# Two weight loads, fifteen narrow matmuls and a table split moved in a retention-plus-feed-forward kernel

## The chip, the core and the metric

The kernel runs on one core of a Trainium2 chip. The metric is the device time of one execution in microseconds (us). Three executions of the kernel before took 202.52, 202.65 and 206.85 us; their median is 202.65 us.

## The reference

Two parts follow each other. The first is a recurrent attention with a decaying state, for 4 batches, 8 heads, 768 steps and a head size of 64. The second is a feed-forward layer over its 3072 rows, with a slope `alpha` for negative values.

```python
gamma = 1 - 2 ** (-5 - arange(H))
for t in range(S):
    state = gamma * state + outer(k[:, :, t], v[:, :, t])
    y[:, :, t] = scale * (q[:, :, t] @ state)
x = y.transpose(0, 2, 1, 3).reshape(3072, 512)
h = x @ w_in                                   # 512 -> 2048
out = (maximum(h, 0) + alpha * minimum(h, 0)) @ w_out   # 2048 -> 512
```

## The kernel before, in words

The 3072 rows are cut into twelve units of 256 rows (three to a batch), and two units make a block, so there are six blocks. Five engines run their own instruction lists in the written order and wait for each other by semaphores: TensorE (PE), VectorE (DVE), ScalarE (ACT), GpSimd (POOL) and SyncE (SP). The schedule is written out by hand: the order of the calls in the source is the order on each engine.

For one unit, `load` (L129) issues DMAs for k, q and v from SP. `rescale` (L166) multiplies k or q by powers of gamma and writes fp16 tiles `kdq`; `cast_v` (L179) makes `vx` from v. Either runs on the engine that the call names (V is DVE, G is POOL). `turn_pe` (L191, through PE and ACT) or `turn_dma` (L187, a transposing DMA from SP) gives the transposed `kq`. `sum_mm` (L218) forms the sums of k times v, `state_sum` (L245) and `state_copy` (L259) the running state `tg`. `score_mm` (L272) multiplies k by q, `masks` (L293) masks the result on DVE, and `out_mm` (L310) multiplies states and masked scores into `y`, which `take_y` (L351) copies out as `xT`.

A block of two units then goes through `ffn1` (L393): sixteen tiles of 128 columns of `w_in`, each four matmuls deep over a moving operand of 512 columns. For the first `apart` tiles the two units go separately, with 256 columns each, two tiles to a bank; a matmul of 256 columns is called narrow here. ACT makes `hm` from each finished bank, DVE combines both into `gt`. Block 0 ends in a plain product `ffn2` (L436), whose four stores are issued from SP at L459 as soon as each result is copied out; later blocks use a product of seven half-size parts (`ffn2_seven`, L462), for which `w_sums` (L370) builds sums of `w_out` quarters once, and `g_sums` (L380) sums of `gt` for each block. Both `ffn` functions are generators: `tick(gen, m)` (L569) issues m more matmuls of one, and this is how the attention of the next units is woven between them.

The weights are loaded from POOL's own DMA queue, in four pieces each: `get_wi(lo, hi)` (L577) and `get_wo(i)` (L581). The DMA converts them from fp32 to fp16. One piece of `w_in` holds four tiles. `behind` (L105) makes one instruction wait for another; `hold` (L115) makes the next plain load wait for the instruction that was last put into `held`.

`SPLIT` (L41) is the unit from which another layout is used: rows of a pair of steps lie 64 apart instead of next to each other. From there on, k and v are loaded by four DMAs each, in rows of 64 numbers instead of 128 (L139 to L147, which does not go through `hold`), half of the score and value matmuls have 64 columns instead of 128 (L282, L336), and the masks have 384 columns instead of 512 (L296).

At the start, DVE rescales unit 0 (L617 to L620), POOL casts its v (L621), issues the first piece of `w_in` (L622) and rescales half of unit 1's q (L623). The second piece is issued at L646, behind POOL's share of the state. `ffn1` of block 0 begins at L668 with seven narrow matmuls ahead of unit 1's `out_mm` (L677).

Of the kernel before, what the change touches and what calls it, by code (L numbers as in the profile page):

```python
# [12 lines left out]
SUB = mybir.AluOpType.subtract  # L13
# [8 lines left out]
def kernel(  # L22
# [10 lines left out]
    nc = tc.nc  # L33
# [4 lines left out]

    SPLIT = 6  # L41
    U = 256
    UPB = S // U
    NU = B * UPB
# [42 lines left out]
    HF, HM = NFT // 2, d_model // 2  # L87
# [5 lines left out]
    def keep(m, bank=7):  # L93
        pt = ps(bank, "kps")
        for i in range(m):
            nc.tensor.matmul(
                out=pt, lhsT=spin[:, 0:128], rhs=spin, start=True, stop=True
            )
# [1 line left out]
    tgbuf = [sbp.tile([128, NP, 128], F16, tag=f"tg{i}", name=f"tg{i}") for i in range(6)]  # L100

    staged, prepped, live, tgs, xT, gts, gsums = {}, {}, {}, {}, {}, {}, {}
    held = []

    def behind(ins, other):  # L105
        tc.add_manual_dep(
            ins.ins,
            other.ins.name,
            mybir.DependencyInfo(
                mybir.DependencyClass.Sync, mybir.DependencyReason.DATA  # L110
            ),
            reason="one engine of two at the second read port",
        )

    def hold(ins):  # L115
# [50 lines left out]
    def rescale(eng, u, t, h0, h1):  # L166
        kdq = unit(u)[0]
        at = OQ if t else (O2 if u >= SPLIT else 0)
        return eng.tensor_tensor(  # L169
            out=kdq[:, t, :, h0:h1, :].rearrange("p r h d -> p h r d"),  # L170
            in0=staged[u]["kq"[t]][:, h0:h1, :].rearrange("p h (r d) -> p h r d", r=2),
            in1=tab[:, at + 2 * h0 : at + 2 * h1]
            .rearrange("p (h r) -> p h r", r=2)
            .unsqueeze(3)
            .to_broadcast([128, h1 - h0, 2, D]),
            op=MULT,
        )

    def cast_v(eng, u, h0=0, h1=H):  # L179
        o = unit(u)[2][:, h0:h1].rearrange("p h r d -> p (h r d)")  # L180
        i = staged[u]["v"][:, h0:h1].rearrange("p h x -> p (h x)")
        if eng is nc.scalar:
            eng.activation(out=o, in_=i, func=COPY, bias=0.0, scale=1.0)
        else:
            eng.tensor_copy(out=o, in_=i)  # L185

    def turn_dma(u):  # L187
        kdq, kq, _ = unit(u)
        nc.sync.dma_start_transpose(out=kq, in_=kdq.rearrange("p t r h d -> p (t r h d)"))
# [51 lines left out]
    def state(u, c, eng, copy="gg"):  # L241

        state_copy(state_sum(u, c, eng), copy)
# [49 lines left out]
    def masks(u, hh, parts=(0, 1)):  # L293
        for a in parts:
            m2 = sbp.tile([128, 512], F16, tag=f"m2{a}{hh}", bufs=2, name=f"m2{a}{hh}")
            if u >= SPLIT:  # L296
                i = nc.vector.tensor_tensor(
                    out=m2[:, 0:384], in0=live[u, hh][a][:, 0:384], in1=mj, op=MULT
                )
            else:  # L300
                i = nc.vector.tensor_tensor(  # L301
                    out=m2.rearrange("p (r a i) -> p r a i", r=2, a=2),
                    in0=live[u, hh][a].rearrange("p (r a i) -> p r a i", r=2, a=2),
                    in1=mask.unsqueeze(2).to_broadcast([128, 2, 2, 128]),
                    op=MULT,
                )
            live[u, hh][a] = m2
        return i
# [58 lines left out]
                scale=1.0,  # L367
            )

    def w_sums(i, lo, hi):  # L370

        w = w_out_all.rearrange("p (k f) (j e) -> p k f j e", k=2, j=2)
        w12, w21, w22 = w[:, 0, lo:hi, 1, :], w[:, 1, lo:hi, 0, :], w[:, 1, lo:hi, 1, :]
        t1, t2, t3, t4 = (wsum[:, x, lo:hi, :] for x in range(4))
        o, a, b = (
            (t1, w12, w[:, 0, lo:hi, 0, :]), (t2, w22, t1), (t3, w22, w12), (t4, w21, t2)
        )[i]
        return nc.vector.tensor_tensor(out=o, in0=a, in1=b, op=SUB)

    def g_sums(n, i, lo, hi):  # L380

# [54 lines left out]
    def ffn2(n, banks, parts=1):  # L436
        gt = gts.pop(n)
        opss = {}
        step = NFT // parts
        for f0 in range(0, NFT, step):  # L440
            for tq in range(4):
                if f0 == 0:
                    opss[tq] = ps(banks[tq % len(banks)], "ops")
                for ft in range(f0, f0 + step):
                    nc.tensor.matmul(  # L445
                        out=opss[tq],
                        lhsT=gt[:, ft, 128 * tq : 128 * tq + 128],
                        rhs=w_out_all[:, ft, :],
                        start=(ft == 0),
                        stop=(ft == NFT - 1),  # L450
                    )
                    if ft == NFT - 1:
                        tag = ("os", "cu")[tq % 2]
                        os_sb = sbp.tile([128, d_model], FP, tag=tag, bufs=3, name=tag)
                        nc.scalar.activation(
                            out=os_sb, in_=opss[tq], func=COPY, bias=0.0, scale=1.0
                        )
                        row = TB * n + 128 * tq
                        nc.sync.dma_start(out=out[row : row + 128, :], in_=os_sb)  # L459
                    yield  # L460

    def ffn2_seven(n, x, y, z=None):  # L462
# [106 lines left out]
    def tick(gen, m=10**6):  # L569
        for _ in range(m):  # L570
            if next(gen, 1) == 1:
                return
# [4 lines left out]
    def get_wi(lo, hi):  # L577
        s = slice(128 * lo, 128 * hi)
        return nc.gpsimd.dma_start(out=w_in_all[:, :, s], in_=wi[:, :, s])
# [37 lines left out]
    rescale(V, 0, 0, 0, 4)  # L617
    rescale(V, 0, 1, 0, 4)
    rescale(V, 0, 0, 4, 8)
    rescale(V, 0, 1, 4, 8)  # L620
    cast_v(G, 0)  # L621
    get_wi(0, 4)  # L622
    rescale(G, 1, 1, 0, 4)  # L623
    keep(10)
    turn_pe(0, 0, 0)
    keep(2)
# [16 lines left out]
    state(0, 0, V, "aa")  # L643
    masks(0, 1, (1,))
    s01 = state_sum(0, 1, G)
    held.append(get_wi(4, 8))  # L646
    load(2, ("k0", "q0", "k1", "q1", "v"))
    rescale(V, 1, 0, 4, 8)
    rescale(V, 1, 1, 4, 8)
# [15 lines left out]
    score_mm(1, 1, (0, 1))  # L665
    masks(1, 1)
    state(1, 1, G)
    gen = ffn1(0, (2, 3, 6, 7, 0, 1, 2, 3, 6, 7, 4, 5, 0, 1, 2, 3), apart=4)  # L668
    tick(gen, 7)
    get_wo(0)  # L670
    rescale(G, 2, 0, 0, 4)
    get_wo(1)
    rescale(G, 2, 1, 0, 4)
    rescale(G, 2, 0, 4, 8)
    rescale(G, 2, 1, 4, 8)
    cast_v(G, 2)
    out_mm(1, (4, 5), evict=False)  # L677
    take_y(1, (0,))
# [7 lines left out]
    turn_pe(2, 0, 5)  # L686
    tick(gen, 5)
    score_mm(2, 0, (6, 7))
    held.append(masks(2, 0, (0,)))
    load(3, ("k0", "q0", "k1", "q1", "v"))  # L690
    masks(2, 0, (1,))
    turn_pe(2, 1, 4)
    tick(gen, 6)
    score_mm(2, 1, (6, 7))
# [3 lines left out]
    held.append(get_wo(2))  # L698
    load(4)
    load(5)  # L700
    rescale(V, 3, 0, 0, 4)
    rescale(G, 3, 1, 0, 4)
    get_wo(3)
    rescale(V, 3, 0, 4, 8)
    rescale(G, 3, 1, 4, 8)
    cast_v(G, 3)
    w_sums(0, 0, HF)
    tick(gen, 9)
    out_mm(2, (4, 5))
    tick(gen, 7)  # L710
# [11 lines left out]
    tick(gen, 8)  # L722
    score_mm(3, 1, (4, 5))
    masks(3, 1)
    state(3, 1, G)
    for f in (0, 4):
        for i in range(1, 4):
            gate = w_sums(i, f, f + 4)
    behind(rescale(G, 4, 1, 0, 8), gate)
    rescale(G, 5, 0, 0, 8)  # L730
    rescale(G, 5, 1, 0, 8)
    cast_v(G, 4)
    cast_v(G, 5)
    tick(gen, 8)
    out_mm(3, (6, 7))
    tick(gen)
    turn_dma(4)
    turn_dma(5)
    load(6)
    tick(half)  # L740
# [2 lines left out]
    for n in range(1, NBLK):  # L743
        more = n + 1 < NBLK
        u0 = 2 * (n + 1)
        if n > 1:
            gen = ffn1(n, (7, 2, 3, 1, 0, 6, 5, 4, 7, 1, 0, 4, 5, 6, 7, 1))
            if more:
                for u in (u0, u0 + 1):
                    i = rescale(G, u, 0, 0, 8)  # L750
                    if u == u0:
                        behind(i, gate)
                    rescale(G, u, 1, 0, 8)
                    turn_dma(u)
                    cast_v(G, u)
                    if u + 2 < NU:
                        load(u + 2)
                    tick(gen, 8)
            tick(gen)
        gen = ffn2_seven(n, 0, 1) if more else ffn2_seven(n, (0, 3), 1, 2)  # L760
        if more:
            tick(gen, 8)
            sum_mm(u0, (2, 3))
            sum_mm(u0 + 1, (2, 3), half=1)
            score_mm(u0, 0, (4, 5))
            score_mm(u0, 1, (6, 7))
            state(u0, 0, G)
            masks(u0, 0)
            s01 = state_sum(u0, 1, G)
            masks(u0, 1, (0,))  # L770
            s10 = state_sum(u0 + 1, 0, G)
            masks(u0, 1, (1,))
            tick(gen, 8)
            state_copy(s01, "aa")
            state_copy(s10)
            tick(gen, 17)
            if n == 1:
                load(7)
            state(u0 + 1, 1, G)
            g_sums(n, 2, 0, HF)  # L780
            tick(gen, 15)
            out_mm(u0, (4, 5))
            score_mm(u0 + 1, 0, (6, 7))
            score_mm(u0 + 1, 1, (2, 3))
            masks(u0 + 1, 0)
            masks(u0 + 1, 1)
            gate = g_sums(n, 3, 0, HF)
            tick(gen, 32)
            out_mm(u0 + 1, (4, 5))
        else:  # L790
            tick(gen, 33)
            g_sums(n, 2, 0, HF)
            g_sums(n, 3, 0, HF)
        tick(gen)
# [30 lines left out]
```

## Time and profile before

| | value |
|---|---|
| median of three executions | 202.65 us |
| the profiled execution | 203.15 us |
| its span in the profile | 201.4 us |
| DVE busy | 155.3 us (77%) |
| ACT busy | 102.0 us (51%) |
| POOL busy | 85.1 us (42%) |
| HBM read, written | 27.31 MB, 6.29 MB |
| granted clock of TensorE | 1.00 |

The profiled execution is 1.75 us longer than its span (what lies before the first and behind the last instruction), and 0.5 us longer than the median. Times inside the profile are counted from the start of the span. An arrow `a <- b` in a list of waits means that a waited for b. L17 or the like is a line of the kernel before.

### The profile page before, as it was taken

Reading aid. Unit: us, or ns where it says so; the run is one execution under the profiler, and the core shown is the slowest. Engines: PE = TensorE matmul, PEld = TensorE weight load, DVE = VectorE, ACT = ScalarE, POOL = GpSimd, SP = SyncE. Lnnn points to the kernel's source line nnn. Section 1 sums busy time; section 2 is a strip of 40 time slices with the busy share of each in tenths; the row PEclk is TensorE's granted clock in tenths of the full one; section 3 lists DMA queues with packets and bytes.
Section 4 is the critical chain, followed back from the end, with each engine's and each line's share of the span. In section 5 each row is a group of like instructions: output and inputs, shape, how many; then the busy total and the mean of one; then the engine's idle time right before and its main releaser. Section 6 shows DMA issues by size and latency. Waiting matters only on the chain.

```text
span 201.4 us, 5574 instructions
## 1 busy us (share of the span) xinstructions
PE 193.2 (96%) x2325; PEld 129.0 (64%) x2325; DVE 155.3 (77%) x251; ACT 102.0 (51%) x170; POOL 85.1 (42%) x99
## 2 busy tenths in 40 slices
PE   6896999999999999999999999999999999999993
PEld 2455644577467778744788644788544888544882
DVE  7695887657799999189997389994489984589851
ACT  2455776348276433477354377334476255466321
POOL 6189029282459463970076950176920250000000
PEclk9999999999999999999999999999999999999999
DMA  6999999499999997998976499992570011300014
GB/s 170 312 230 148 205 251 260 136 245 198 339 344 136 215 222 180 240 277 221 213 188 162 157 178 240 198 225 87 175 160 0 3 53 55 107 0 0 14 41 156
DMA packets 77561, 33.95 MB, mean 169 GB/s; under 512 B 43217, under 2 KB 77025, under 8 KB 77537
## 3 DMA queue, kind: packets, MB, share of 16 engines
q1 hardware_dynamic: 73136, 29.37, 56.8%
q0 software_dynamic: 4224, 4.19, 13.4%
q8 instruction: 18, 0.29, 0.6%
q10 hardware_dynamic: 176, 0.04, 0.1%
q14 instruction: 7, 0.05, 0.1%
HBM read 27.31 MB, written 6.29 MB: 167 GB/s over the span
## 4 chain that ended last, share of the span: by engine, by line
PE 86%; DMA 6%; DVE 2%; POOL 2%; SPq 1%; issue 1%; ACT 0%; POOLq 0%
PE hps L407 41%; PE ox L493 16%; PE oy L493 11%; PE ops L445 7%; DMA win<-in_moe_w_in_dram 4%; PE y L339 3%; DMA vs<-in_v_dram 3%; PE y L319 2%; PE sca L284 2%; SPq L149 1%; PE st L229 1%; PE trb L199 1%; PE oz L493 1%; DVE gs L391 1%; POOL tf L255 1%
## 5 line engine op out<-in xcount | busy, mean ns | idle before, releaser
L407 PE MATMUL hps<-xT,win 128*128 128x512 f16 (+1 forms) x448 | 84.7, 349 | 1.6 <-DMA win<-in_moe_w_in_dram 1.6
L420 DVE SCALAR_TENSOR_TENSOR gt<-hm,oma,hps 128x512 f16<-128x512 f32 (+1 forms) x112 | 71.1, 668 | 10.2 <-ACT hm L418 4.9
L418 ACT ACTIVATE hm<-hps 128x512 f32<-128x512 f32 x96 | 57.2, 597 | 32.2 <-PE hps L407 29.7
L407 PEld LDWEIGHTS <-win 128*128 128x128 f16 x448 | 43.5, 98 | 40.2 <-DMA win<-in_moe_w_in_dram 1.7
L493 PEld LDWEIGHTS <-gs 128*128 128x128 f16 x320 | 31.0, 98 | 3.8
L255 POOL TENSOR_TENSOR tf<-ss,tab 128x256 f32<-128x256 f32 x16 | 12.2, 764 | 36.2 <-DVE ss L254 35.3
L493 PEld LDWEIGHTS <-gt 128*128 128x128 f16 x240 | 22.8, 98 | 4.6
L509 ACT ACTIVATE cu<-ox 128x512 f32<-128x512 f32 (+1 forms) x18 | 9.5, 527 | 29.3 <-PE ox L493 29.2
L169 POOL TENSOR_TENSOR kdq<-ks,tab 128x1024 f16<-128x1024 f32 (+1 forms) x10 | 17.3, 1729 | 15.6 <-DMA ks<-in_k_dram 8.4
L514 DVE TENSOR_TENSOR os<-oy,cu 128x512 f32<-128x512 f32 x14 | 9.6, 689 | 17.2 <-PE oy L493 13.5
L169 POOL TENSOR_TENSOR kdq<-qs,tab 128x1024 f16<-128x1024 f32 (+1 forms) x13 | 21.3, 1641 | 2.8 <-issue 1.9
L270 POOL CAST tg<-tf 64x256 f16<-64x256 f32 x27 | 13.2, 491 | 19.6 <-DVE tf L251 18.3
L493 PE MATMUL ox<-wsum,gs 128*128 128x256 f16 x160 | 19.1, 273 | 0.0
L362 ACT ACTIVATE xT<-y 128x512 f16<-128x512 f32 x23 | 15.7, 743 | 6.0 <-PE y L339 5.8
L445 PE MATMUL ops<-wout,gt 128*128 128x512 f16 x64 | 15.3, 380 | 0.0
L185 POOL CAST vx<-vs 128x1024 f16<-128x1024 f32 (+1 forms) x13 | 12.5, 971 | 4.1 <-DMA vs<-in_v_dram 4.1
L391 DVE TENSOR_TENSOR gs<-gt 128x1024 f16<-128x1024 f16 (+1 forms) x14 | 13.1, 934 | 0.3
L268 ACT ACTIVATE tg<-tf 64x256 f16<-64x256 f32 x13 | 5.3, 414 | 14.0 <-POOL tf L255 9.0
L205 ACT ACTIVATE kq<-trb 128x1024 f16<-128x1024 f16 x8 | 8.2, 1024 | 7.1 <-PE trb L199 7.0
L301 DVE TENSOR_TENSOR m<-sca,mi 128x512 f16<-128x512 f32 x12 | 8.2, 687 | 3.4 <-PE scb L284 3.4
L493 PE MATMUL ox<-wout,gt 128*128 128x256 f16 x80 | 10.4, 274 | 0.0
L445 PEld LDWEIGHTS <-gt 128*128 128x128 f16 x64 | 5.8, 98 | 6.0
(55 smaller groups left out, 190.7 us busy)
## 6 DMA issues: line engine op xcount, KB each, us to landing
out_dram<-os SPq DMA_DIRECT2D x21, 256.0 KB, 3.0
qs<-in_q_dram SPq DMA_DIRECT2D x8, 512.0 KB, 5.7
ks<-in_k_dram SPq DMA_DIRECT2D x24, 128.0 KB, 3.5
vs<-in_v_dram SPq DMA_DIRECT2D x24, 128.0 KB, 4.8
ks<-in_k_dram SPq DMA_DIRECT2D x8, 256.0 KB, 4.8
qs<-in_q_dram SPq DMA_DIRECT2D x8, 256.0 KB, 5.1
win<-in_moe_w_in_dram POOLq DMA_DIRECT2D x4, 512.0 KB, 7.8
wout<-in_moe_w_out_dram POOLq DMA_DIRECT2D x4, 512.0 KB, 8.1
```

The source lines that it names most:

```text
L169: return eng.tensor_tensor(out=kdq[:, t, :, h0:h1, :].rearrange("p r h d -> p h r d"), in0=staged[u]["kq"[t]][:, h0:h1, :].rearrange("p h ...
L185: eng.tensor_copy(out=o, in_=i)
L255: eng.tensor_tensor(out=t, in0=ss, in1=dec, op=MULT)
L270: nc.gpsimd.tensor_copy(out=o, in_=i)
L362: nc.scalar.activation(out=o, in_=i, func=COPY, bias=0.0, scale=1.0,)
L391: return nc.vector.tensor_tensor(out=o, in0=a, in1=b, op=op)
L407: nc.tensor.matmul(out=hps[:, f, :].rearrange("p (u t) -> p u t", t=U), lhsT=w_in_all[:, hp, 128 * (f0 + f) : 128 * (f0 + f) + 128], rhs=x ...
L418: nc.scalar.activation(out=hm, in_=hps, func=RELU, bias=0.0, scale=-1.0)
L420: nc.vector.scalar_tensor_tensor(out=gt[:, f0 + f, U * lo : U * hi], in0=hm[:, f, :], scalar=oma_sb[:, f0 + f : f0 + f + 1], in1=hps[:, f, :],
L445: nc.tensor.matmul(out=opss[tq], lhsT=gt[:, ft, 128 * tq : 128 * tq + 128], rhs=w_out_all[:, ft, :], start=(ft == 0), stop=(ft == NFT - 1),)
L493: nc.tensor.matmul(out=o[1][m], lhsT=lhs(f, m), rhs=rhs(f), start=(first and f == 0 and (m == 0 or o[0] is None)), stop=(f == HF - 1), ski ...
L514: nc.vector.tensor_tensor(out=so, in0=o[0], in1=t, op=ADD)
```

## The change

Nothing of the computation changes but the layout of units 4 and 5. In short: the layout of `SPLIT` begins at unit 4; the first piece of `w_in` is issued ahead of POOL's cast of unit 0's v, once DVE's fourth rescale is done, and the second right behind POOL's first rescale; fifteen instead of seven narrow matmuls stand ahead of unit 1's `out_mm`, and six instead of four tiles go unit by unit; unit 3's loads wait for unit 2's last rescale instead of a mask; unit 3's rescales all run on POOL, as does the first `w_sums`; block 0's stores go behind unit 4's transpose; the last state of unit 3 is copied by ACT, later; unit 5's rescale of q goes behind two casts; and in the loop one mask goes ahead of a state sum.

```diff
-    SPLIT = 6
+    SPLIT = 4
...
-    held = []
+    held, late = [], []
...
-    def w_sums(i, lo, hi):
+    def w_sums(i, lo, hi, eng=nc.vector):
...
-        return nc.vector.tensor_tensor(out=o, in0=a, in1=b, op=SUB)
+        return eng.tensor_tensor(out=o, in0=a, in1=b, op=SUB)
...
-                        nc.sync.dma_start(out=out[row : row + 128, :], in_=os_sb)
+                        late.append((out[row : row + 128, :], os_sb))
...
     rescale(V, 0, 0, 4, 8)
-    rescale(V, 0, 1, 4, 8)
+    i = rescale(V, 0, 1, 4, 8)
+    behind(get_wi(0, 4), i)
     cast_v(G, 0)
-    get_wi(0, 4)
     rescale(G, 1, 1, 0, 4)
+    held.append(get_wi(4, 8))
     keep(10)
...
     s01 = state_sum(0, 1, G)
-    held.append(get_wi(4, 8))
     load(2, ("k0", "q0", "k1", "q1", "v"))
...
-    gen = ffn1(0, (2, 3, 6, 7, 0, 1, 2, 3, 6, 7, 4, 5, 0, 1, 2, 3), apart=4)
-    tick(gen, 7)
+    gen = ffn1(0, (2, 3, 6, 7, 0, 1, 2, 3, 6, 7, 4, 5, 0, 1, 2, 3), apart=6)
+    tick(gen, 15)
...
-    rescale(G, 2, 1, 4, 8)
+    held.append(rescale(G, 2, 1, 4, 8))
+    load(3, ("k0", "q0", "k1", "q1", "v"))
     cast_v(G, 2)
...
-    held.append(masks(2, 0, (0,)))
-    load(3, ("k0", "q0", "k1", "q1", "v"))
-    masks(2, 0, (1,))
+    masks(2, 0)
...
-    rescale(V, 3, 0, 0, 4)
-    rescale(G, 3, 1, 0, 4)
+    for h in (0, 4):
+        rescale(G, 3, 0, h, h + 4)
+        rescale(G, 3, 1, h, h + 4)
     get_wo(3)
-    rescale(V, 3, 0, 4, 8)
-    rescale(G, 3, 1, 4, 8)
     cast_v(G, 3)
-    w_sums(0, 0, HF)
+    w_sums(0, 0, HF, G)
...
-    state(3, 1, G)
+    s31 = state_sum(3, 1, G)
...
     rescale(G, 5, 0, 0, 8)
-    rescale(G, 5, 1, 0, 8)
     cast_v(G, 4)
     cast_v(G, 5)
+    rescale(G, 5, 1, 0, 8)
     tick(gen, 8)
     out_mm(3, (6, 7))
     tick(gen)
+    state_copy(s31, "aa")
     turn_dma(4)
+    for o, t in late:
+        nc.sync.dma_start(out=o, in_=t)
     turn_dma(5)
...
             masks(u0, 1, (0,))
+            masks(u0, 1, (1,))
             s10 = state_sum(u0 + 1, 0, G)
-            masks(u0, 1, (1,))
```

More of the change, by code (lines that the diff above doesn't have):

```diff
@@ L111, in behind @@
             ),
-            reason="one engine of two at the second read port",
+            reason="in turns",
         )
```

## The prediction

> **What bounds the kernel now.** I read the page's slices first, then the chain of waits in order of time, then PE's waits, then the DMA queues in short windows.
>
> ```profile
> PE 193.2 (96%) x2325; PEld 129.0 (64%) x2325; DVE 155.3 (77%) x251; ACT 102.0 (51%) x170; POOL 85.1 (42%) x99
> PE   6896999999999999999999999999999999999993
> ...
> DMA  6999999499999997998976499992570011300014
> ```
>
> PE is full from the fourth slice to the last but one, at full clock. A gain must come out of the first 18 us, out of PE's few waits, or out of PE's own work. The chain at the start:
>
> ```profile
> 3.50 5.41 DMA vs<-in_v_dram
> ...
> 9.07 0.99 POOL vx L185
> 10.06 7.61 DMA win<-in_moe_w_in_dram
> 17.67 0.05 issue
> 17.72 0.94 PE hps L407 x7
> ```
>
> Unit 0's v lands, POOL casts it, only then is w_in's first piece issued, and it lands 7.61 us later. PE's list of waits:
>
> ```profile
> PE hps L407 <- DMA win<-in_moe_w_in_dram: 1.6, 1, 1.6
> ...
> PE y L339 <- DVE m L301: 0.4, 1, 0.4
> ```
>
> The first is at 16.15 to 17.72; the second at 74.3, in block 1.
>
> **Part 1, the first two pieces of w_in.** DVE's fourth rescale ends at 8.15, so POOL issues piece one at 8.2 instead of 10.06: 1.85 earlier. The issue costs POOL 0.94, so the cast starts at 9.15 instead of 9.07; its reader, `sum_mm(0)`, starts at 10.27, which hides 0.08. The rescale of unit 1's q follows at 10.5 instead of 11.03, and saves PE at most the 0.23 that it waited at 12.13, most of it covered by the state copies on ACT that end at 12.46. Piece two is issued at about 11.6 instead of 13.54. If pieces simply landed as much earlier, piece one would come at 15.8, PE would start at 16.15, when its scores are done, and the gain would be 1.57.
>
> The DMA engines say otherwise. The same view of queues, for 10.2 to 12, then 12.05 to 13.5, then 24.5 to 28 (packets, MB, share of 16 engines):
>
> ```profile
> q1 hardware_dynamic: 1065, 0.53, 103.7%
> ```
> ```profile
> q0 software_dynamic: 109, 0.11, 59.1%
> q1 hardware_dynamic: 370, 0.18, 41.5%
> ```
> ```profile
> q0 software_dynamic: 513, 0.51, 85.7%
> q1 hardware_dynamic: 477, 0.24, 33.7%
> ```
>
> q1 holds SP's loads, q0 the weights. Until 12 the engines are full with unit 1's loads, which end at 13.64. In the second window a load packet still takes 41.5% x 16 x 1.45 / 370 = 26 ns, what it takes alone; the weights come in only as engines run dry. The same at 42.7 to 44.7, 1.9 us long: 606 load packets at 26 ns beside 176 of weights. So packets that are queued first go first, for at least these 1.9 us, some 70 packets an engine. At 10.2, piece one's new arrival (issue plus the 2 us between issue and first packet), 1468 load packets are left until 13.7, 92 an engine: most of them go ahead of it. Then w_in starts hardly earlier; what goes is the ramp at 12 to 13.4. And piece two, at 20.97 before, now counts: six tiles unit by unit put tile 4, from piece two, right after the sixteenth narrow matmul, where before 32 came first. At 163 packets a us (309 in the 1.9 us from 13.5) the 1024 packets of both pieces take 6.3 us from 12.8 on average; with 0.6 for the slowest engine and 0.3 to report that is 20.0, by the 178 a us of 18 to 24 19.5; the dips of the trace would add up to 0.5. PE, started at about 16.6, does fifteen narrow ones (1.63 at 0.109), `out_mm` (1.0 to 1.2) and one more by 19.5, and then waits until 20.2. Before, PE reached that amount of work at 17.72 + 2.85 = 20.6. I take a gain of 0.5, with bounds of 1.57 and, by the second rival, a loss of 2.0.
>
> [...]
>
> **Part 2, fifteen narrow matmuls, six tiles.** `out_mm(1)` needs the state copied at 17.56, 1.7 behind `sum_mm(1)`; with PE at 16.6, seven narrow ones would leave it waiting 0.2, fifteen do not. Eight wide matmuls become sixteen narrow ones: 64 wide took 13.81 (0.216 each), 24 narrow 2.62 (0.109), so nothing on PE. DVE pays four halves at 0.476 instead of two results at 0.747, 0.4 in all; in the wide tiles that follow PE gives it 0.86 each and it needs 0.75, so four of them make it good.
>
> **Part 3, block 1.** Block 4 (units 10 and 11) has the same place in its batch as block 1 (units 4 and 5), and the new layout. From the end of `ffn1` to the start of the next, block 1 takes 83.80 - 67.04 = 16.76, block 4 172.15 - 156.41 = 15.74. The 1.02 holds the 0.43 that PE waited for a mask at 74.72. That mask was queued behind a state sum, which waited for POOL; it now goes ahead of it, and the four masks take 0.55 instead of 0.69. Behind the mask now wait that sum and unit 5's state, read at 78.9, over 2 us later than it is made. Gain 1.0, bounds 0.5 (the layout alone) and 1.0.
>
> **Part 4, what is moved and hidden.** Unit 2's loads wait for piece two, as before, and unit 3's for POOL's last rescale (33.9 before) instead of a mask at 36.6: both earlier, 4 us of cover for their readers at 33.6 and 45.5. POOL takes over two rescales (2 x 1.05) and a `w_sums`: the trace has none on POOL; 1.22 on DVE below, 3.6 above, from rescales (1.05 for 512, 1.90 for 1024 columns, so 0.85 per 512). I take 3.6, the nearer row. POOL was idle for 6.82 ahead of 53.23; 5.7 fits. Queued behind it are the state copy of unit 3 and unit 4's rescale. Without that cover 1 to 2 us of POOL's lateness reach block 1. DVE loses 2.6 us of work before 46, none on the path.
>
> Units 4 and 5 load in rows of 256 bytes: 0.72 MB in 2.5 us (66 to 68.5) against 2.01 MB in 6 us (50 to 56), so 3.15 MB take 10.9 instead of 9.4: 1.5 more. SP issues eighteen DMAs instead of six, 0.65 each. Against this, unit 4's k no longer waits for w_out's third piece (the four-part loads skip `hold`), and that piece no longer shares the engines with unit 3. v of unit 5 must land by about 64; it did at 60.4. Casting ahead of the last rescale gives PE its v two us before 67.83, where POOL finished at 67.79 before; and unit 5's transpose starts at 67.8 instead of 65.84. Landing takes 4.5 (median), its reader is at 74.87: 2.5 of slack. The four stores pass behind unit 4's transpose on SP while unit 5's rescale is awaited. Unit 6's loads and the first store of block 1 slip by 2 us; the reader of unit 6's k is at 80.15, it lands near 74. Two state copies move to ACT (2 x 0.41), ahead of `hm` tiles whose spacing of 0.86 leaves 0.26 free each. All at nothing; without covers up to 2 us.
>
> **Sum.** The span 201.4 - 0.5 - 1.0 = 199.9; plus 1.75 outside it 201.65 against the profiled 203.15; the median lies 0.5 lower: 201.1 us.
>
> **Rivals.**
> First, weights for free: the pieces land as early as they are issued. For it: piece one moves from 12.05 to 17.67, at half the bytes a us of the loads. Against it: the full engines until 13.4. Gain 1.57 + 1.0: 200.1 us.
>
> Second, taking turns at once. Its place is unit 1's v, the last of the loads. A pair of packets took 3.5 x 16 / 495 = 0.113 us at 24.5 to 28. From 10.2, 64 pairs for two pieces take 7.2, then 28 load packets 0.7, then 0.3: v lands at 18.5 instead of 13.64. Cast 0.6, second half of the sums 0.3, scores 0.3: PE starts `ffn1` at 19.7, 2.0 later, and with 1.0 from block 1 the time is 203.65 us. It decides from v landing later than about 15, and becomes a loss over the whole kernel from 17.5. Turns from the seventieth packet on give v at 16 to 17 and about the forecast.
>
> Third, POOL or SP late for block 1: `w_sums` stretched, or transposes and loads crowded, by up to 3 us beyond the slack of 2 to 2.5. For it: POOL finished 0.04 ahead of PE's need before. Against it: two casts now come first. 1 to 3 us on the forecast: 202 to 204.
>
> Fourth, no start gain at all: the first pieces land as before. 201.6 us, inside the forecast's own spread.
>
> **From cases to numbers.** Forecast with the fourth (200.6 to 201.9) 0.55; first 0.18; second 0.15; third 0.09; others 0.03. The predicted time is the forecast's, 201.1. From 199.8 to 203.7 the range holds the first, the second at its price and most of the third. A measurement of this kernel can tell about 2% from no change. Faster by over 2% needs 198.6, 1.5 below the first rival: 0.03. Slower by over 2% needs 206.7, the second and third together: 0.05. Within: 0.92.
>
> **What would show it.** Right: PE's wait on w_in at the start shrinks to under 1 us and part of it comes back behind the sixteenth narrow matmul; packets of q1 stay at 26 ns until they end near 13.5; no PE wait for a mask, and block 1 takes 15.7. The second rival: unit 1's cast of v after 17, q1's packets near 40 ns from 10 on. The third: PE waits for `vx`, `kq` or `tg` at 65 to 75. Wrong altogether: a PE wait after 75, or a span under 198.5.

## The result: a loss that begins in the first 18 us

| | before | after |
|---|---|---|
| median of six executions each | 203.01 us | 205.80 us |
| ratio, 95% interval | | 1.0133 [1.0094, 1.0173] |
| the profiled execution | 203.15 us | 203.90 us |
| its span | 201.4 us | 202.2 us |

The kernel became 1.3% slower, by an interval that lies clear of 1, and its time lies above the predicted 199.8 to 203.7 us. The ratio leaves out executions in a slower state, the medians do not. Single executions lie far apart (202.1 to 206.9 us before, 203.9 to 207.3 us changed), and the profiled one is the fastest of the changed kernel's six, so its trace shows the mildest form of what happened; a second trace of the same kernel, the first experiment, shows it in full.

The page of the changed kernel, first busy times, then the slices:

```profile
PE 192.0 (95%) x2333; PEld 129.1 (64%) x2333; DVE 151.2 (75%) x250; ACT 102.8 (51%) x172; POOL 89.9 (44%) x100
PE   6786999899999999999999999999999999999993
PEclk9999999999999999999999999999999999999999
DMA  5999999599979969799899699991560011200004
```

PE has less to do than before (192.0 against 193.2 us), and the span is longer: what was lost is waiting. The third and fourth slices of PE (10 to 20 us) read 8 and 6, where they read 9 and 6, and the eighth has a new dent. PE's list of waits names them (the waiting operation, the one waited for, us in total, times, longest):

```profile
PE st L229 <- POOL vx L185: 2.1, 2, 1.6
...
PE trb L199 <- POOL kdq L169: 1.0, 1, 1.0
PE y L319 <- ACT tg L268: 0.5, 1, 0.5
PE sca L284 <- DMA kq<-kdq: 0.3, 1, 0.3
```

Both waits of the page before, for `w_in` (1.57) and for a mask (0.43), are gone. In place of the first stands a wait for `vx`, unit 1's v. The timelines of PE and then of POOL in this trace (start, duration, instruction, in brackets the idle time before it and who ended it):

```profile
16.91 0.32 PE L229 MATMUL st<-vx,kdq 64*64 64x64 f16 x16 [1.63 <-POOL vx L185]
17.39 1.81 PE L407 MATMUL hps<-xT,win 128*128 128x256 f16 x15
...
36.94 0.40 PE L199 MATMUL trb<-mi,kdq 128*128 128x128 f16 x4 [0.99 <-POOL kdq L169]
...
105.04 0.24 PE L284 MATMUL sca<-kq 64*64 64x128 f16 x1 [0.34 <-DMA kq<-kdq]
```
```profile
8.08 0.96 POOL L579 DMA_DIRECT2D win<-in_moe_w_in_dram  x1 [3.10 <-DVE kdq L169]
...
11.52 0.81 POOL L579 DMA_DIRECT2D win<-in_moe_w_in_dram  x1
...
16.25 0.62 POOL L185 CAST vx<-vs 128x512 f16<-128x512 f32 x1 [1.63 <-DMA vs<-in_v_dram]
```

The weights were issued when the prediction said (8.08 and 11.52), and piece one was there before PE asked for it. But the second half of unit 1's v, which landed at 13.64 before, landed at 16.2. Cast, second half of the sums and scores follow it, and `ffn1` starts at 17.39 instead of 17.72: 1.57 of waiting for weights became 1.63 of waiting for v. The DMA queues of the changed kernel at 12 to 14 and at 14 to 16 (packets, MB, share of 16 engines) show why:

```profile
q0 software_dynamic: 331, 0.34, 99.6%
q1 hardware_dynamic: 170, 0.09, 20.6%
```
```profile
q0 software_dynamic: 288, 0.28, 84.3%
q1 hardware_dynamic: 367, 0.18, 34.3%
```

Before, 403 load packets (q1) passed at 12 to 14 and none after. Now 170 pass there and 367 wait until 14 to 16, behind 331 and then beside 288 packets of weights. In the first window a load packet takes 20.6% x 16 x 2 / 170 = 39 ns instead of 26, and one of weights 99.6% x 16 x 2 / 331 = 96 ns.

The rest of the profiled execution: `ffn1` of block 0 starts 0.33 earlier, the last half of block 0's `ffn2` ends 0.92 later, block 1 gives 0.94 back (its stage takes 15.82 instead of 16.76), the next stage loses 0.48 and the last copies 0.3. That is -0.33 + 1.25 - 0.94 + 0.48 + 0.3 = 0.8, the difference of the spans. The chain of waits names the transfers behind two of these:

```profile
20.59 15.18 DMA qs<-in_q_dram
35.84 1.05 POOL kdq L169
36.94 0.40 PE trb L199 x4
...
99.77 5.23 DMA kq<-kdq
```

Unit 2's last half of q was issued earlier than before, as forecast, but landed at 35.8 instead of 32.15, because `w_out`'s second piece, issued at 26.90 instead of 30.03, shared the engines with it: at 32 to 35, 419 packets of weights passed beside 386 of loads. And SP issued unit 7's transpose at 99.77 instead of 95.56. SP's timeline of the changed kernel, with the transposes of units 5, 6 and 7:

```profile
68.58 1.61 SPq L189 DMA_TRANSPOSE kq<-kdq  x1
...
88.56 3.15 SPq L189 DMA_TRANSPOSE kq<-kdq  x1
...
99.77 3.23 SPq L189 DMA_TRANSPOSE kq<-kdq  x1
```

Before they were issued by 65.84, at 86.44 and at 95.56: SP, 2.7 late at the first, is 4.2 late at the third.

### The profile page after: what moved, and what is told of

Read it like the earlier page. It is cut to its first block, busy times and chain, and to the rows that moved or that the text cites. A ratio compares the mean times of both kernels' runs of the same rounds, so it can differ in the third digit from the quotient of the medians.

```text
span 202.2 us, 5608 instructions
## 1 busy us (share of the span) xinstructions
PE 192.0 (95%) x2333; PEld 129.1 (64%) x2333; DVE 151.2 (75%) x250; ACT 102.8 (51%) x172; POOL 89.9 (44%) x100
## 4 chain that ended last, share of the span: by engine, by line
PE 73%; DMA 16%; POOL 3%; DVE 3%; issue 2%; SPq 2%; ACT 1%; POOLq 0%
PE hps L407 34%; PE ox L493 14%; PE oy L493 11%; DMA qs<-in_q_dram 10%; PE ops L445 6%; DMA win<-in_moe_w_in_dram 4%; DMA kq<-kdq 3%; PE y L339 2%; PE y L319 2%; SPq L149 2%; PE sca L284 1%; POOL kdq L169 1%; DVE gs L391 1%; PE oz L493 1%; PE st L229 1%
## 5 line engine op out<-in xcount | busy, mean ns | idle before, releaser
L420 DVE SCALAR_TENSOR_TENSOR gt<-hm,oma,hps 128x512 f16<-128x512 f32 (+1 forms) x114 | 70.9, 660 | 15.3 <-ACT hm L418 10.5
L407 PEld LDWEIGHTS <-win 128*128 128x128 f16 x456 | 44.3, 98 | 37.7
L255 POOL TENSOR_TENSOR tf<-ss,tab 128x256 f32<-128x256 f32 x16 | 11.4, 710 | 33.8 <-DVE ss L254 33.4
L493 PEld LDWEIGHTS <-gt 128*128 128x128 f16 x240 | 22.8, 98 | 4.5
L169 POOL TENSOR_TENSOR kdq<-ks,tab 128x1024 f16<-128x1024 f32 (+1 forms) x12 | 19.4, 1616 | 13.4 <-DMA ks<-in_k_dram 7.7
L169 POOL TENSOR_TENSOR kdq<-qs,tab 128x1024 f16<-128x1024 f32 (+1 forms) x13 | 20.7, 1594 | 6.7 <-DMA qs<-in_q_dram 3.6
L270 POOL CAST tg<-tf 64x256 f16<-64x256 f32 x25 | 12.6, 504 | 14.5 <-DVE tf L251 13.3
L445 PE MATMUL ops<-wout,gt 128*128 128x512 f16 x64 | 15.3, 380 | 0.0
L268 ACT ACTIVATE tg<-tf 64x256 f16<-64x256 f32 x15 | 6.2, 415 | 16.1 <-POOL tf L255 10.4
L185 POOL CAST vx<-vs 128x1024 f16<-128x1024 f32 (+1 forms) x13 | 13.1, 1008 | 2.3 <-DMA vs<-in_v_dram 2.0
L254 DVE TENSOR_TENSOR ss<-tf,st 128x256 f32<-128x256 f32 x16 | 6.6, 413 | 4.8 <-PE st L229 4.4
L493 PE MATMUL oy<-wsum,gs 128*128 128x256 f16 x80 | 9.6, 273 | 0.1
```

What stands on the lines that cost most here:

```text
L169: return eng.tensor_tensor(out=kdq[:, t, :, h0:h1, :].rearrange("p r h d -> p h r d"), in0=staged[u]["kq"[t]][:, h0:h1, :].rearrange("p h ...
L255: eng.tensor_tensor(out=t, in0=ss, in1=dec, op=MULT)
L270: nc.gpsimd.tensor_copy(out=o, in_=i)
L407: nc.tensor.matmul(out=hps[:, f, :].rearrange("p (u t) -> p u t", t=U), lhsT=w_in_all[:, hp, 128 * (f0 + f) : 128 * (f0 + f) + 128], rhs=x ...
L420: nc.vector.scalar_tensor_tensor(out=gt[:, f0 + f, U * lo : U * hi], in0=hm[:, f, :], scalar=oma_sb[:, f0 + f : f0 + f + 1], in1=hps[:, f, :],
L445: nc.tensor.matmul(out=opss[tq], lhsT=gt[:, ft, 128 * tq : 128 * tq + 128], rhs=w_out_all[:, ft, :], start=(ft == 0), stop=(ft == NFT - 1),)
```

## The experiments

Three explanations stood at first. The one that the expectations below call the theory took the loss from unit 2's q and `w_out`'s second piece, the 0.99 of PE at 36.94. Its first rival was the start: unit 1's v is what the early weights delay, and by more in the median than in the profiled execution. The second was SP, late at unit 7's transpose. The start is what the runs bore out. Ratios are to the kernel before, run beside them.

**after_again: the changed kernel once more.**

> The changed kernel once more, for a second trace. Its profiled execution was 203.90 us, but the undisturbed executions beside it 205.5 to 205.9: the trace explains only 0.8 us of span. Theory (unit 2's loads): with piece two landing at 18.7 instead of 21.0 they start earlier, run against three pieces of weights in turns, and how late they end differs between executions; a trace at 205 or more then shows PE waiting 2 to 3 us ahead of unit 2's transposes near 36 us, where the first showed 0.99. Rival (the start): unit 1's v is later than in the first trace, and PE waits 3 us or more ahead of 17 us, where it waited 1.63. Rival (SP late): unit 7's transposed tile makes PE wait 2 us near 105 us, where it waited 0.34.

205.39 us, 1.0129 [1.0056, 1.0203]. The traced execution took 209.07 us. PE's timeline in it:

```profile
17.56 0.32 PE L229 MATMUL st<-vx,kdq 64*64 64x64 f16 x16 [1.96 <-POOL vx L185]
22.32 0.43 PE L229 MATMUL st<-vx,kdq 64*64 64x64 f16 x16 [4.44 <-POOL vx L185]
```

Here even the first half of v came late, and the second landed only at 21.6. The DMA view of 19 to 21.5 in the same trace shows what was still moving then:

```profile
q0 software_dynamic: 23, 0.02, 5.5%
q1 hardware_dynamic: 21, 0.01, 2.1%
```

Both queues together use 7.6% of 16 engines, the time of 1.2 of them, and share it about evenly: 23 packets of weights and 21 of loads in 2.5 us, 0.114 us for a pair. At 12 to 14 the same queues had used 114% (100.4% and 13.9%). That v waited for the last packets of one engine or two is my estimate from the 1.2; no view tells the engines apart. The loss then grows by the clock. Windows of one microsecond in this trace (window, its length, PE busy and other engines, then the granted clock, DMA share and GB/s as the last three):

```profile
18.00:19.00 1.00, 0.00 (x0) 0.00 (x0) 0.00 (x0) 0.00 (x0) 0.00 (x0) 0.84 0.20 32
19.00:20.00 1.00, 0.00 (x0) 0.00 (x0) 0.00 (x0) 0.00 (x0) 0.00 (x0) 0.50 0.08 14
...
24.00:25.00 1.00, 1.00 (x7) 0.69 (x6) 0.83 (x2) 0.41 (x1) 0.98 (x2) 0.50 1.16 309
25.00:26.00 1.00, 1.00 (x9) 0.83 (x8) 0.34 (x1) 0.60 (x1) 0.91 (x3) 0.75 1.18 219
```

While PE stood still the clock fell to half (0.84 at 18 to 19, 0.50 at 19 to 20), and it was 0.50 up to 25 and 0.75 on the mean of 25 to 26, so about 3.2 us at half after PE had started again at 22.32. The fifteen narrow matmuls at 23.10 took 2.97 instead of the first trace's 1.81. By estimate the half clock costs about 1.6 us, half of the 3.2. The sum agrees with the first trace: 202.2 + (6.8 - 2.1) of waiting for `vx` + 1.6 - 1.0 = 207.5, where 207.4 was measured. The 1.0 taken off is the wait at 36.94, which is not there at all in this execution, and the time is the longest. So unit 2's loads fell as the main cause.

**b_win: the kernel before with the start of the change alone.**

```diff
-    rescale(V, 0, 1, 4, 8)
+    i = rescale(V, 0, 1, 4, 8)
+    behind(get_wi(0, 4), i)
     cast_v(G, 0)
-    get_wi(0, 4)
     rescale(G, 1, 1, 0, 4)
+    held.append(get_wi(4, 8))
...
-    held.append(get_wi(4, 8))
...
-    gen = ffn1(0, ..., apart=4)
-    tick(gen, 7)
+    gen = ffn1(0, ..., apart=6)
+    tick(gen, 15)
```

> The kernel before with the start alone: the first piece of w_in ahead of the cast, the second behind POOL's first rescale, fifteen narrow matmuls, six tiles unit by unit. Theory (unit 2's loads): unit 2's loads start at 18.7 here too, so the loss is all here: 1.3% slower than before or more (there is no gain in block 1 to set against it), 205.5 to 207 us, PE waits 1 us or more near 36 us. Rival (the rest is to blame, SP or POOL late): no slower than before by more than 0.3 us, 202.5 to 203.3.

205.75 us, 1.0153 [1.0089, 1.0217]. The first two parts of the change are enough for the whole loss, and PE waits nowhere near 36 us. PE in its trace, and the clock right after:

```profile
18.65 0.43 PE L229 MATMUL st<-vx,kdq 64*64 64x64 f16 x16 [3.20 <-POOL vx L185]
```
```profile
20.00:21.00 1.00, 1.00 (x7) 0.70 (x5) 1.00 (x3) 0.41 (x1) 0.93 (x3) 0.50 0.67 32
```

**b_split: the kernel before with the layout and the order of the mask alone.**

```diff
-    SPLIT = 6
+    SPLIT = 4
...
+            masks(u0, 1, (1,))
             s10 = state_sum(u0 + 1, 0, G)
-            masks(u0, 1, (1,))
```

> The kernel before with the layout from unit 4 on and the mask ahead of the state sum, nothing else. Block 1 takes 15.75 us instead of 16.76 from the end of the first product to the start of the next, as in the changed kernel (83.79 - 67.97). If the loads of units 4 and 5 in rows of 256 bytes cost nothing, the time is 1.0 us less than before, 202.0; if they make PE wait near 67 or 75 us, that wait is taken off.

204.51 us, 1.0117 [1.0059, 1.0174]: a loss as well, in another place.

```profile
69.24 0.26 PE L284 MATMUL sca<-kq 64*64 64x128 f16 x1 [1.83 <-DMA kq<-kdq]
```
```profile
70.00:71.00 1.00, 1.00 (x10) 0.73 (x6) 1.00 (x4) 0.00 (x0) 0.76 (x2) 0.50 0.86 193
```

With more and shorter loads but the old order, unit 4's transposed tile lands only at 69.2, PE waits 1.83, and the clock is 0.67 on the mean of 69 to 70, 0.50 from 70 to 72 and 0.62 at 72 to 73. In the changed kernel this wait is absent. So part 3's gain did not come without part 4; which of part 4's moves of loads, rescales and stores covers the layout no run here separates.

**a_wo: the changed kernel with `w_out`'s second piece two rescales later.**

```diff
     rescale(G, 2, 0, 0, 4)
-    get_wo(1)
     rescale(G, 2, 1, 0, 4)
     rescale(G, 2, 0, 4, 8)
+    get_wo(1)
```

> The changed kernel with w_out's second piece issued two rescales later, behind unit 2's second rescale of k. Theory (unit 2's loads): in the first trace that piece was issued at 26.9, in the middle of unit 2's loads, and took turns with their second half, which ended at 35.8 and 37.3; without it they end near 32 and PE does not wait near 36: 1 us less in a trace like the first, 1.5 to 2.5 less in the typical execution, so 203 to 204.3. Rival (start or SP late): within 0.5 us of the changed kernel. A new wait could come for w_out's second piece, near 39 us.

204.12 us, 1.0086 [1.0046, 1.0125]. The wait at 36.94 is gone, and another has come for the piece itself; v is late as before:

```profile
17.27 0.32 PE L229 MATMUL st<-vx,kdq 64*64 64x64 f16 x16 [2.22 <-POOL vx L185]
```
```profile
39.08 1.24 PE L445 MATMUL ops<-wout,gt 128*128 128x512 f16 x5 [0.66 <-DMA wout<-in_moe_w_out_dram]
```

Whether it gains anything isn't settled: the interval overlaps that of the changed kernel. It does not bring the kernel back to 1.

**a_win_back, a_win1, a_win2: the pieces apart.** In a_win_back both pieces stand in their old places, all else as changed; in a_win1 only piece one is early; in a_win2 only piece two. One diff shows all three; the comment names the kernels that have the line.

```diff
     i = rescale(V, 0, 1, 4, 8)
-    behind(get_wi(0, 4), i)          # a_win_back, a_win2
     cast_v(G, 0)
+    get_wi(0, 4)                     # a_win_back, a_win2
     rescale(G, 1, 1, 0, 4)
-    held.append(get_wi(4, 8))        # a_win_back, a_win1
...
     s01 = state_sum(0, 1, G)
+    held.append(get_wi(4, 8))        # a_win_back, a_win1
```

> The changed kernel with both early pieces of w_in back in their old places (behind the cast; behind POOL's share of the state), all else as changed. Theory (v in turns with weights): unit 1's v lands near 13.6 us again, PE's wait for its cast goes from 1.6 to 4.4 us down to about 0.2, the executions stand close together again, and what the rest of the change brings is seen: block 1 about 0.9 us shorter, 0.3 us lost at unit 7's transpose: 201.5 to 202.5 us with before at 202.5, so no slower and up to 0.5% faster. Rival (the rest is also slow: loads, SP, POOL): still 0.5% slower or more, 203.5 us or above.

> The changed kernel with only the second piece of w_in back in its old place; the first stays ahead of the cast. Theory: the first piece alone shares turns with the last loads, 32 packets an engine, and ends before the second begins, so v lands between 13.6 and 16.5 and PE waits for its cast 0.3 to 1.8 us; the worst executions (4 us of wait, lower granted clock) are gone: 202.5 to 204. If the first piece were all of it: like the changed kernel, 205.5. If it were nothing: like the kernel with both back, and better by what the earlier landing brings.

> The changed kernel with the first piece of w_in back behind the cast, and the second still behind POOL's first rescale (issued near 12.1 instead of 13.5). Theory: the second piece's packets begin behind the first's, when the loads have ended at 13.6, so no turns with v: as the kernel with both back, within 0.3%, unit 2's loads a little earlier. If the second piece alone were the cause: 204 to 206 us and PE waits 1.5 us or more for the cast.

| | median us | ratio | interval |
|---|---|---|---|
| a_win_back | 203.41 | 1.0055 | 1.0021 to 1.0089 |
| a_win1 | 205.25 | 1.0170 | 1.0145 to 1.0194 |
| a_win2 | 202.96 | 1.0042 | 1.0022 to 1.0062 |

Piece one does it, alone. In a_win_back's trace the wait for v is 0.23, as before the change, but `w_in` itself came late: PE waited 2.55 for it until 19.06, the next fifteen narrow matmuls took 3.30 instead of 1.81, and the granted clock of the page's fourth and fifth slices (15.3 to 25.5) reads 8 and 7 tenths. The kernels with piece one in its old place differ there from trace to trace, from 0.47 (b_split) to 2.64 (a_back_order) of waiting for `w_in`, so one trace alone does not price the start. The traces of a_win1 and then a_win2:

```profile
17.07 0.32 PE L229 MATMUL st<-vx,kdq 64*64 64x64 f16 x16 [1.66 <-POOL vx L185]
```
```profile
16.40 1.81 PE L407 MATMUL hps<-xT,win 128*128 128x256 f16 x15 [0.81 <-DMA win<-in_moe_w_in_dram]
...
103.80 0.24 PE L284 MATMUL sca<-kq 64*64 64x128 f16 x1 [1.25 <-DMA kq<-kdq]
```

In a_win2 PE doesn't wait for v (the thirty-two matmuls of its sums run without a gap from 14.42), and `ffn1` starts at 16.40, 1.32 earlier than before. What is left over 1 shows further on: 1.25 of waiting for unit 7's `kq`.

**a_vfirst: the changed kernel with unit 1's v loaded ahead of the second halves of its k and q.**

```diff
-    load(1, ("k0", "q0", "k1", "q1", "v0", "v1"))
+    load(1, ("k0", "q0", "v0", "v1", "k1", "q1"))
```

> The changed kernel with unit 1's v loaded ahead of its second halves of k and q, so that these are the last of the loads. Theory (whatever load is last shares turns with the weights): v lands by 12.5 and the wait for its cast goes; the second half of q lands at 16 to 21 instead, DVE's rescale of it and the transposes behind it make PE wait 2 us or more ahead of unit 1's second transposes: as slow as the changed kernel or slower, 205 to 208 us. Rival (it is POOL's cast that is slow, not the landing): PE's wait shrinks, 202 to 204 us.

207.31 us, 1.0280 [1.0221, 1.0340]. Now the wait stands at the rescaled k and q:

```profile
18.03 0.56 PE L199 MATMUL trb<-mi,kdq 128*128 128x128 f16 x4 [3.91 <-DVE kdq L169]
```

Here the loads that come last pay, with 3.91 of waiting instead of 1.63; those two are also needed earlier than v, and by longer work.

**The order of SP: a_back_order, a_win2_order, after_order, and a_back_casts.** The first three take a_win_back, a_win2 and the changed kernel, and let SP issue the transposes of both units of a block ahead of the following loads. The fourth is a_win_back with unit 5's rescale of q ahead of the two casts, as in the kernel before.

```diff
-                    if u + 2 < NU:
+                    if u > u0 and u + 2 < NU:
+                        load(u + 1)
                         load(u + 2)
```
```diff
     rescale(G, 5, 0, 0, 8)
+    rescale(G, 5, 1, 0, 8)           # a_back_casts
     cast_v(G, 4)
     cast_v(G, 5)
-    rescale(G, 5, 1, 0, 8)           # a_back_casts
```

> The changed kernel with both pieces of w_in back in their old places, and in the loop both units' transposes issued from SP ahead of the two following units' loads (not: transpose, loads, transpose, loads). With the pieces back alone it was 0.55% slower than before. Theory (SP late gives block 1's gain back): SP reaches unit 7's transpose at 98 to 100 instead of 95.6, so PE waits 0.3 to 1.25 us near 104; with the transpose ahead of unit 8's loads it is issued near 92, the wait goes, and the time is 0.3 to 1.2 us less than with the pieces back alone: 201.4 to 202.6, level with before or up to 0.5% faster. Rival (the first tiles of w_in land late at random): no change, 0.3 to 0.8% slower than before.

> The same order of transposes with only the first piece of w_in back, the second still behind POOL's first rescale, which alone was 0.42% slower than before, with 1.25 us of PE's wait near 104 in its trace. Theory: that wait goes, 1.0 to 1.3 us in a trace like that: 201 to 202, 0 to 0.6% faster than before. Rival (the start): no change.

> The changed kernel with that order of transposes alone, both early pieces of w_in as changed. Theory (the two costs add): the start keeps its loss of about 0.8% to 1.1%; the order brings 0.3 to 0.5 us, as PE arrives late at unit 7's scores anyway: 204 to 205.5, 0.8 to 1.3% slower than before. If the order were the whole cause: level with before.

> The changed kernel with both pieces of w_in back, and unit 5's rescale of q ahead of the two casts again, as before. Theory (SP late): unit 5's transpose is issued 2 us sooner, near 66.5 instead of 68.6, all that follows on SP too, and unit 7's transpose near 97 to 98: PE's wait near 104 goes or falls under 0.3; PE may wait up to 0.3 for unit 5's v near 67. 201.5 to 203, 0 to 0.4% slower than before. If the two casts' place does not matter: 0.55% slower, as without.

| | median us | ratio | interval |
|---|---|---|---|
| a_back_order | 202.35 | 0.9991 | 0.9963 to 1.0018 |
| a_win2_order | 201.75 | 0.9935 | 0.9898 to 0.9971 |
| after_order | 204.58 | 1.0074 | 1.0033 to 1.0116 |
| a_back_casts | 202.36 | 0.9996 | 0.9974 to 1.0018 |

The order is worth 0.6% to 1.1% in the three pairs; the intervals of a_win2 and a_win2_order are well apart, those of the changed kernel and after_order overlap. After_order keeps the start's loss: its trace has 3.34 of waiting for v ahead of 19.69, and a clock of 0.50 from 19 to 25 and of 0.65 at 25 to 26. a_win2_order beats both kernels, by 0.65% against the one before. The transposes of units 6 and 7 in its trace, and PE's start:

```profile
85.14 5.34 SPq L189 DMA_TRANSPOSE kq<-kdq  x2
```
```profile
16.84 1.81 PE L407 MATMUL hps<-xT,win 128*128 128x256 f16 x15 [0.80 <-DMA win<-in_moe_w_in_dram]
```

PE waits nowhere for a transpose. In a_back_casts, where piece two is issued late as in the kernel before, the six tiles unit by unit show the wait behind the sixteenth narrow matmul that the prediction described, 0.54 ahead of 20.45; in a_win2_order it is absent.

## Why the prediction was wrong, point by point

**The step that failed** is in part 1: "packets that are queued first go first, for at least these 1.9 us, some 70 packets an engine". From it followed that unit 1's loads would end where they ended before, and a gain of 0.5. The two windows it was read from, 12.05 to 13.5 and 42.7 to 44.7, have more loads than weights, and I took this for a rule of order. The first shows only how weights begin: in the trace before, their first microsecond (12 to 13) has 40 of their packets beside 361 of loads, and in the changed kernel's (10.5 to 11.5) 40 beside 578. What came then breaks the rule. From 11.5 to 13, with 510 packets of loads still to come, 279 packets of weights passed and only 75 of loads; from 13 to 14 the two queues took turns, 140 and 143, with 39 to 40 ns for a load packet instead of 26; and the end of unit 1's v, 367 packets that came after 14, finished last, at 16.2 instead of 13.64. Why the weights first pass nearly alone, no run here tells. That `ffn1` started 0.33 earlier in the profiled execution, near the 0.5 of the forecast, is luck: the wait for weights had become one for v.

**The second rival** (chance 0.15) had the mechanism, the place and the price of a pair: 0.113 forecast, 0.114 measured at 19 to 21.5 in after_again. Its turns were read from 24.5 to 28 of the trace before, with 513 packets of weights against 477 of loads. The trace of the changed kernel agrees with them at 13 to 14 (140 against 143), and at 11.5 to 13 the loads got even less than by turns (75 against 279). I set 12.05 to 13.5 of the trace before against it (109 against 370), and that window shows only means over sixteen engines. Even the rival missed two points. It had v at one time, 18.5, or at 16 to 17 with late turns "and about the forecast"; the traces spread over 16.2, 17.9 (b_win) and 21.6, and no run shows why. And it priced only the wait.

**The clock was in no case of mine.** After waits of 3.20 (b_win), 3.91 (a_vfirst), 3.34 (after_order) and 4.44 (after_again) windows of one microsecond read a clock of 0.50, and it was back at 1.00 some 3.3, 3.5, 6.0 and 3.2 us after PE had started again, as I estimate from the mean of the window in which it changed (0.55, 0.73, 0.65 and 0.75). The fifteen narrow matmuls there took 3.00, 2.36, 3.38 and 2.97 instead of 1.81. The length of the wait alone does not decide: 1.83 was enough in b_split, and 2.55 in a_win_back, while 2.64 in a_back_order was not. The mean granted clock of the changed kernel's five other executions was 0.982 to 1.00, below 0.995 in four of them, so they are like after_again rather than like the profiled one. That their waits are the same ones is inferred, since only traced executions show waits. Over all runs such a mean clock, below 0.995, goes with the early first piece: 30 of 41 executions of the kernels that have it (the changed one, b_win, a_wo, a_win1, a_vfirst, after_order), 8 of 58 of the other changed kernels, and 5 of 63 of the kernel before that ran beside them.

**SP** is the second error, in part 4. "Unit 5's transpose starts at 67.8 instead of 65.84 ... 2.5 of slack" held for unit 5 (68.58, and PE doesn't wait there). It was counted for that reader alone: "Unit 6's loads and the first store of block 1 slip by 2 us" should have been followed to the end of SP's list, where the lateness grew to 4.2 and met unit 7's transpose. "Wrong altogether: a PE wait after 75" is what came. The wait is 0.34 in the profiled execution and 0.28 to 1.25 in a_wo, a_win1, a_win2, a_vfirst and a_back_casts; it is missing in after_again, where PE itself is 4 us late, and in a_win_back's trace. Either remedy, the order on SP or the old place of the rescale, takes a_win_back from 1.0055 to 1.00. For the order, a_win2 and a_win2_order show the wait of 1.25 going with the time. For the old place of the rescale the cause is not shown: in a_back_casts unit 7's transpose was issued at 96.70 instead of 99.77, and PE still waited 0.60 for it.

**What held.** Part 3: block 1 takes 15.82 instead of 16.76, against 15.74 forecast, and no mask is waited for. Part 2: the narrow matmuls cost PE nothing. Of part 4, `w_sums` on POOL took 4.07 (3.6 assumed, 1.22 on DVE) and is hidden; the third rival's waits at 65 to 75 did not come. "4 us of cover" for unit 2's q did not hold in the first trace (0.99 of waiting); in after_again and b_win it did. The forecast's sum, 1.5 off the time, was nearly reached by a_win2_order (0.65% by its ratio, 1.3 us of 202.65), but not by the forecast's route: that kernel is without the early first piece and has another order on SP.

**Left open.** How the loss of those other executions divides into waiting and clock; why the second half of v lands at 16.2 in one execution of the changed kernel and at 21.6 in another; and whether a_wo is worth something once the start is mended.

## What to carry to other kernels

Before a transfer is moved ahead, find the load that will be last in flight beside it, and follow its readers: here 170 load packets passed at 12 to 14 instead of 403, and unit 1's v landed at 16.2 and at 21.6 instead of 13.64. A list of DMAs that one engine issues in order has to be followed to its last entry; slack at the next reader says little of the third: SP was 2.7 late at unit 5's transpose, where PE did not wait, and 4.2 late at unit 7's, where it did. And a wait of PE is priced with what the clock does after it: by estimate 1.6 us behind the 4.44 of after_again, nothing behind the 2.64 of a_back_order.

## What was not expected of the hardware

In after_again the transfers all but stopped with a load still in flight: the DMA share was 0.20 at 18 to 19 and 0.06 to 0.08 from 19 to 22, against 1.16 at 24 to 25, and POOL waited 4.14 for the second half of v before it cast it at 21.65. At 19 to 21.5 all traffic was 44 packets, 23 of weights and 21 of loads, and PE, DVE and ACT were idle from 18 to 22.

The granted clock halved around PE's waits of 1.83 in b_split (0.50 at 70 to 72) and 2.55 in a_win_back (fifteen narrow matmuls in 3.30), but not around 2.22 in a_wo (1.00 on the mean of 10 to 20.7 and of 20.7 to 26) or 2.64 in a_back_order (9 tenths in every slice of its page, fifteen narrow matmuls in 1.81). What tells them apart, no run here shows.
